# Attention and ELU MLP on one Trainium2 core: PSUM banks given out by hand, and column sums moved into score banks

## The chip, the core and the metric

One core of a Trainium2 chip runs the whole program. TensorE (PE in the profile) multiplies matrices into PSUM, which holds eight banks of 128 partitions by 512 fp32 columns; VectorE (DVE) and ScalarE (ACT) read and write PSUM, GpSimd (POOL) works on SBUF, and SyncE (SP) issues the transfers. The metric is the device time of one launch in microseconds (us), median of several runs.

## The reference

Eight batches, twelve heads, 448 positions, head width 64; then an MLP over all 3584 tokens.

```python
q_n, k_n = rmsnorm(q, g_q), rmsnorm(k, g_k)
scores = scale * np.matmul(q_n, k_n.transpose(0, 1, 3, 2))
attn = np.exp(scores - np.max(scores, axis=-1, keepdims=True))
attn = attn / (np.sum(attn, axis=-1, keepdims=True) + 1e-09)
x = np.matmul(attn, v)          # heads side by side: 3584 x 768
h = x @ w_in                    # 768 x 2048
g = np.where(h > 0.0, h, np.exp(np.minimum(h, 0.0)) - 1.0)
return g @ w_out                # 2048 x 768
```

## The kernel before

The kernel works in fp16 pairs: every operand is split into a high part and the rest of it (`hi` and `lo`), so most products are three or two matmuls.

**Order of the work.** The program is written out in half steps `h` by one loop at its end, and no scheduler reorders it: each engine gets its instructions in the order in which the loop emits them. A chunk `T` is 128 rows of scores of a pair of heads; there are 7 chunks to a pair, 6 pairs to a batch, so 42 chunks (`PB`) to a batch, and two half steps to a chunk. Around half step 2T stand, for chunk T and the chunks behind it: `s_mm` (L533, scores of chunk T+1, two or four matmuls into a bank), `s_max` (L540, VectorE, row maximum), `s_exp` (L546, ScalarE, exponential in place, with row sums), `s_z` (L550, GpSimd), `s_rec` (L557, VectorE), `s_hi` (L564, ScalarE) and `s_lo` (L569, VectorE), which reads the bank last. After that SyncE transposes the probabilities by DMA (`s_tr`, L579), and once per pair `attend` (L590, 22 matmuls into the bank `av`) multiplies them with v. `x_high` (L597, ScalarE) and `x_low` (L601, VectorE) take the result out of `av`.

**Stages.** In batch 0 there is attention only. From half step 92 on the MLP of batch b-1 (L676 and L690) is spread over the attention of batch b, and the MLP of the last batch stands alone at the end.

**Weights.** In the first two batches the fp32 weights are split: 16 blocks of w_in (`conv_in`, half steps up to 83) and 24 blocks of w_out (`conv_out`, half steps 60 to 150). A block goes through ScalarE (L224, L225), a join on VectorE (L230, L256), **column sums** on PE (L129: 9 or 13 matmuls of 64 columns with a matrix of ones), the largest of them on VectorE (`largest`, L132), and from that a scale. For w_in there follow `dgw` (L279, ScalarE), `whi` (L282, GpSimd), four matmuls on PE (`s_low`, L289 and L290) and two copies out (`wli`, L293). For w_out there follow GpSimd (L313, L322) and ScalarE (L318). Each batch also has one column sum for the scale of v (`v_steps`). That is 48 column sums in all.

**PSUM.** Four banks (tag `s`) go round for scores, three (tag `mo`) for the MLP, for `s_low` and for the first 23 column sums, and one bank is `av`. The other 25 column sums use columns 448 to 511 of `av`, since a score or an attention result fills only 448 of 512 columns. The framework places the waits: an instruction waits for earlier ones of other engines on the same PSUM tile, and a tile is a whole bank.

Of the kernel before, what the change touches and what calls it, by code (L numbers as in the profile page):

```python
# [8 lines left out]
F32 = mybir.dt.float32  # L9
# [5 lines left out]
ALU = mybir.AluOpType  # L15
AX = mybir.AxisListType
# [3 lines left out]
B, H, S, D = 8, 12, 448, 64  # L20
# [12 lines left out]
def tile_attention_then_elu_mlp(ctx: ExitStack, tc: tile.TileContext, qk, v, v_scan, gg, w_in, w_out, out):  # L33
# [18 lines left out]
    psum = ctx.enter_context(tc.tile_pool(name="psum", bufs=1, space=PSUM))  # L52
    pool = ctx.enter_context(tc.tile_pool(name="pool", bufs=1))

    def pst(tag, bufs):
        return psum.tile([128, 512], F32, tag=tag, name=tag, bufs=bufs)

    def t_s():
        return pst("s", 4)

    av = psum.tile([128, 512], F32, name="av")

    def t_mo():
        return pst("mo", 3)

    ident = const.tile([128, 128], F32, name="ident")
    make_identity(nc, ident)
# [53 lines left out]
    def upper(t):  # L121

        return t.bitcast(BF16).rearrange("p (n w) -> p n w", w=2)[:, :, 1]

    def column_sums(parts, bank):


        for i, a in enumerate(parts + [tiny]):
            nc.tensor.matmul(bank[:, S:], ones, a, start=i == 0, stop=i == len(parts))  # L129

    def largest(bank, e):
        nc.vector.tensor_reduce(out=e, in_=bank[:, S:], axis=AX.X, op=ALU.max)  # L132
        return e

    POWER = 0x7F800000
# [66 lines left out]
    a_out = const.tile([128, NC_], F32, name="a_out")  # L202
    most = const.tile([128, 4 * NC_], F32, name="most")

    def conv(src, i, width, acol, parts, own=True):

        raw = raw_in[i % len(raw_in)] if width == WI_W else room(raws, 2 * width, i)
        raw = raw.rearrange("p (n w) -> p n w", w=2)  # L210

        t, w = room(wts, width, i), room(w32s, width, i if width == WI_W else i + 2)
        ws = bank = None

        def load():
            nc.sync.dma_start(
                out=raw, in_=src[i].bitcast(U32).rearrange("p (n w) -> p n w", w=2)
            )

        def s_act():  # L220

            nc.scalar.activation(t, raw[:, :, 1].bitcast(F32), AF.Abs, scale=2.0**-112)  # L224
            nc.scalar.activation(  # L225
                w.bitcast(I32), raw[:, :, 0], AF.Copy, scale=0.875 * 2.0**-29, bias=0.49
            )

        def s_join():
            nc.vector.scalar_tensor_tensor(  # L230
                out=t.bitcast(U32), in0=t.bitcast(U32), scalar=3, in1=w.bitcast(U32),
                op0=ALU.logical_shift_left, op1=ALU.bitwise_or,
            )

        def s_sums():
            nonlocal bank
            bank = t_mo() if own else av
            column_sums([upper(t[:, a : a + 64]) for a in range(0, width, 64)], bank)

        def s_scale():  # L240
            nonlocal ws
            e = largest(bank, acol)
            ws = small("ws")

            ibits(ws, e, POWER, ALU.bitwise_xor, POWER, ALU.bitwise_and)
            if width == WO_W and i % 12 == 11:
                d = i // 4 - 2
                for r in range(4):
                    rows = slice(32 * r, 32 * r + 32)
                    ibits(  # L250
                        a_out[rows, d : d + 3], most[rows, 4 * d + r : 4 * d + 12 : 4],
                        POWER, ALU.bitwise_and, 0, ALU.bitwise_or,
                    )

        def s_sign():
            nc.vector.scalar_tensor_tensor(  # L256
                out=w.bitcast(U32), in0=raw[:, :, 1], scalar=0x80000000, in1=t.bitcast(U32),
                op0=ALU.bitwise_and, op1=ALU.bitwise_or,
            )

        steps = [
            (-(10, 6, 7)[min(max(i - 2, 0), 2)] if width == WI_W else 0 if i == 1 else -1, load), (3, s_act), (4, s_join), (5, s_sign), (6, on_pe(s_sums)),
            (8, s_scale),
        ]
        for h, fn in parts:
            step = lambda fn=fn: fn(w, ws)
            steps.append((h, on_pe(step) if fn in late else step))
        return steps

    def conv_in(f):  # L270
# [14 lines left out]

        def s_low(w, ws):
            for i, c in enumerate(half):
                pss[i] = t_mo()
                nc.tensor.matmul(pss[i][:, :384], dgw, w[:, c], start=True, stop=False)  # L289
                nc.tensor.matmul(pss[i][:, :384], neg, hi[:, c], start=False, stop=True)  # L290

# [9 lines left out]
    def conv_out(i):  # L301
# [22 lines left out]
        def s_store(w, ws):  # L324
# [1 line left out]

        return conv(
            w_out, i, WO_W, most[:, i : i + 1],
            [(9, s_mult), (10, s_high), (11, s_low), (12, s_store)], own=i < WO_OWN,
        )  # L330


# [129 lines left out]

    def v_steps(b):

        m1 = dg = None

        def one():
            nonlocal m1
# [6 lines left out]
            nc.scalar.activation(dg, ident, AF.Copy, scale=m1)  # L475

        def three():
            column_sums([upper(dg[:, :64]), upper(dg[:, 64:])], av)

        def four():  # L480

            p2 = vpow[b] = small("p2", bufs=4)
            ibits(p2, largest(av, small("mx")), POWER, ALU.bitwise_and, 0, ALU.bitwise_or)
            vs = vscale[b] = small("vs")
            ibits(vs, p2, -1, ALU.mult, (254 + 7 + UP) * E, ALU.add)

# [38 lines left out]

    def s_mm(T):
        p, j = divmod(T, NJ)
        ps = pss[T] = t_s()
        qq = qkt[p].rearrange("p t j n -> p t (j n)")
        for t in (0, 2):  # L530
            for h, r0, q0, n in cuts(ORDER[j]):
# [205 lines left out]
    for b in range(B):  # L737
# [3 lines left out]
            at(h0 + 2 * i + 3, scan_max, b, i)  # L741
        steps_at(h0 + (15 if b else 13), v_steps(b))
        at(HB * (b + 1), m_scale, b)

    for f in range(NF):
        if f < 2:
            first = (
# [71 lines left out]


WO_START = 60
WO_OWN = 7
UP = 13
RATE = 576 / (2 * PB)
X_LAG = 8
# [33 lines left out]
```

## Time and profile before

| what | value |
|---|---|
| median of 3 runs | 1305.69 us (1304.90 to 1305.71) |
| profiled execution: device time | 1306.18 us |
| profiled execution: span of the instructions | 1304.4 us |
| PE busy | 1192.3 us (91%) |
| DVE busy | 875.1 us (67%) |
| ACT busy | 800.5 us (61%) |
| POOL busy | 719.4 us (55%) |

The 1.8 us between the span and the device time lie around the program. Busy shares are means over stages that are limited by different things, so they have to be read stage by stage: PE is busy 2 to 8 tenths of the time in the first 200 us, and over nine tenths from about 250 us to the end.

### The profile page before, as it was taken

The numbers are of one execution on the slowest core, as the hardware profiler recorded it, in microseconds if no ns is written. First come the engines' busy times: TensorE is split into PE (matmuls) and PEld (weight loads), VectorE is DVE, ScalarE is ACT, GpSimd is POOL, SyncE is SP. The second block draws the span as 40 slices with busy tenths as digits, with TensorE's granted clock in tenths as the row PEclk, the third lists the DMA queues.
The fourth block names the chain that finished last, engine by engine and source line by source line (L and its number), as shares of the span: only waits on it lengthen the run. The fifth ranks groups of instructions, "written<-read, shape, count | busy, mean of one in ns | idle before, by whom it ended". The sixth has DMA issues, their size and how long they took to land.

```text
span 1304.4 us, 21596 instructions
## 1 busy us (share of the span) xinstructions
PE 1192.3 (91%) x6976; PEld 716.9 (55%) x6976; DVE 875.1 (67%) x1905; ACT 800.5 (61%) x1761; POOL 719.4 (55%) x1067
## 2 busy tenths in 40 slices
PE   2666558899999999999999999999999999999998
PEld 1323224456655775567556665576556655666576
DVE  6878898987578566866687558756686668642310
ACT  5777777776577566765677457655675467643310
POOL 4676678886465545655566456654665456531100
PEclk9786679999999999999999999999999999999999
DMA  7888887979877795769667986678677966764011
GB/s 251 199 190 209 192 204 180 204 177 202 181 133 147 171 215 128 156 138 238 135 136 151 201 169 133 143 183 199 130 150 146 230 135 148 137 124 107 1 47 61
DMA packets 444881, 208.22 MB, mean 160 GB/s; under 512 B 407136, under 2 KB 421088, under 8 KB 444768
## 3 DMA queue, kind: packets, MB, share of 16 engines
q1 hardware_dynamic: 444768, 206.85, 71.4%
q8 instruction: 55, 0.90, 0.3%
q14 instruction: 58, 0.48, 0.1%
HBM read 93.52 MB, written 14.16 MB: 83 GB/s over the span
## 4 chain that ended last, share of the span: by engine, by line
PE 71%; DMA 3%; DVE 1%; SPq 1%; issue 0%; ACT 0%; ACTq 0%
PE mo L676 29%; PE mo L690 28%; PE s L533 7%; PE av L590 6%; DMA pt<-p 2%; DMA vscan<-in_v_scan 1%; SPq L579 0%; DVE p L569 0%; DMA out<-y 0%; DVE st L540 0%; SPq L429 0%; DVE mv L167 0%; ACT p L564 0%; SPq L162 0%; SPq L665 0%
## 5 line engine op out<-in xcount | busy, mean ns | idle before, releaser
L676 PE MATMUL mo<-x,whi 128*128 128x448 f16 x1536 | 422.9, 353 | 5.7 <-DVE e L623 5.7
L690 PE MATMUL mo<-gall,whos 128*128 128x448 f16 x1536 | 423.0, 353 | 0.1
L540 DVE TENSOR_REDUCE st<-s 128x1 f32<-128x448 f32 x336 | 208.3, 620 | 188.5 <-PE s L533 186.8
L690 PE MATMUL mo<-gall,wls 128*128 128x448 f16 x768 | 272.1, 354 | 0.0
L676 PE MATMUL mo<-x,wli 128*128 128x448 f16 x768 | 271.0, 353 | 0.0
L564 ACT ACTIVATE p<-s,st 128x448 f16<-128x448 f32 x294 | 185.6, 631 | 133.5 <-DMA pt<-p 115.0
L690 PEld LDWEIGHTS <-whos 128*128 128x128 f16 x1536 | 221.6, 145 | 72.5
L546 ACT ACTIVATE s<-s,st 128x448 f32<-128x448 f32 x336 | 203.5, 606 | 87.5 <-DVE st L540 87.3
L550 POOL TENSOR_SCALAR st<-st 128x1 f32<-128x1 f32 x336 | 80.4, 239 | 304.0 <-ACT s L546 283.1
L533 PE MATMUL s<-qkt 128*128 128x448 f16 (+1 forms) x768 | 190.9, 371 | 59.4 <-DVE gall L569 37.9
L676 PEld LDWEIGHTS <-whi 128*128 128x128 f16 x1536 | 150.0, 98 | 144.2 <-issue 7.9
L569 DVE SCALAR_TENSOR_TENSOR p<-s,st,p 128x448 f16<-128x448 f32 x294 | 197.0, 670 | 29.0 <-ACT p L564 27.7
L617 POOL TENSOR_SCALAR e<-e,isc 128x448 f32<-128x448 f32 x128 | 95.2, 743 | 149.8 <-ACT e L614 147.8
L533 PEld LDWEIGHTS <-qkt 128*128 128x128 f16 (+1 forms) x768 | 63.2, 102 | 130.5 <-issue 72.0
L690 PEld LDWEIGHTS <-wls 128*128 128x128 f16 x768 | 110.6, 144 | 42.2 <-issue 7.8
L631 DVE SCALAR_TENSOR_TENSOR gall<-e,gsc,gall 128x448 f16<-128x448 f32 x128 | 104.5, 817 | 23.0 <-ACT gall L628 23.0
L628 ACT ACTIVATE gall<-e,gsc 128x448 f16<-128x448 f32 x128 | 85.4, 667 | 52.3 <-DVE e L623 52.1
L590 PE MATMUL av<-pt,vt 128*64 128x448 f16 x1056 | 112.1, 358 | 5.1 <-DMA pt<-p 5.1
L676 PEld LDWEIGHTS <-wli 128*128 128x128 f16 x768 | 75.0, 98 | 74.7 <-issue 7.5
L623 DVE SCALAR_TENSOR_TENSOR e<-e,mo 128x448 f32<-128x448 f32 x128 | 78.5, 613 | 35.4 <-POOL e L617 35.3
L614 ACT ACTIVATE e<-mo,sc 128x448 f32<-128x448 f32 x128 | 79.9, 624 | 31.2 <-PE mo L676 31.2
L436 POOL COPY qkt<-qkt 64x896 f16<-64x896 f16 x96 | 93.5, 974 | 5.0
(100 smaller groups left out, 1409.8 us busy)
## 6 DMA issues: line engine op xcount, KB each, us to landing
wls<-wl_d SPq DMA_DIRECT2D x48, 512.0 KB, 4.2
nat<-in_qk SPq DMA_DIRECT2D x48, 448.0 KB, 3.7
raws<-in_w_out SPq DMA_DIRECT2D x24, 512.0 KB, 4.2
out<-y SPq DMA_DIRECT2D x48, 224.0 KB, 3.6
vn<-in_v SPq DMA_DIRECT2D x38, 256.0 KB, 3.5
vscan<-in_v_scan SPq DMA_DIRECT2D x36, 224.0 KB, 4.0
whos<-in_w_in SPq DMA_DIRECT2D x10, 768.0 KB, 5.3
pt<-p SPq DMA_TRANSPOSE x336, 3.2
```

The lines of the kernel that those rows point to most:

```text
L436: nc.gpsimd.tensor_copy(out=q[z : z + 64, 2], in_=q[a : a + 64, 0])
L533: nc.tensor.matmul(ps[r0 : r0 + n, :S], lhs, qq[:, 1, h * S : h * S + S], start=(t == 0), stop=(t == 2),)
L540: nc.vector.tensor_reduce(out=st[:, 0:1], in_=pss[T][:, :S], axis=AX.X, op=ALU.max, negate=True)
L546: nc.scalar.activation(ps, ps, AF.Exp, bias=st[:, 0:1], accum_out=st[:, 1:2])
L564: nc.scalar.activation(p16[:, :S], pss[T][:, :S], AF.Copy, scale=stats[T][:, 2:3])
L569: nc.vector.scalar_tensor_tensor(out=p16[:, S:], in0=ps[:, :S], scalar=r, in1=p16[:, :S], op0=ALU.mult, op1=ALU.subtract)
L590: nc.tensor.matmul(av[64 * h : 64 * h + 64, :S], vt[p][:, j + NJ * i, h], pt[h][:, j, :], start=(k == 0), stop=(k == len(terms) - 1),)
L617: nc.gpsimd.tensor_scalar(out=e, in0=e, scalar1=-1.0, scalar2=isc, op0=ALU.add, op1=ALU.mult)
L628: nc.scalar.activation(g[:, 0], e, AF.Copy, scale=gsc)
L631: nc.vector.scalar_tensor_tensor(out=g[:, 1], in0=e, scalar=gsc, in1=g[:, 0], op0=ALU.mult, op1=ALU.subtract)
L676: nc.tensor.matmul(ph[:, :S], w[:, c, :], x[:, r, :], start=(c == 0 and i == 0), stop=last)
L690: nc.tensor.matmul(py[:, :S], w, g[:, r, :], start=(f == 0 and i == 0), stop=last)
```

## The change

All eight banks become fixed tiles: `s0` to `s4`, `av`, `m0` and `m1`. Scores go round five banks in batch 0 and round `s0` to `s3` after it, when `s4` becomes the third MLP bank. `s_low` always uses `m0` and `m1`. Every column sum goes to columns 448 to 511 of one of `s0` to `s3`, in turn, whatever chunk is in that bank.

```diff
-    def pst(tag, bufs):
-        return psum.tile([128, 512], F32, tag=tag, name=tag, bufs=bufs)
-
-    def t_s():
-        return pst("s", 4)
-
-    av = psum.tile([128, 512], F32, name="av")
+    def bank(name):
+        return psum.tile([128, 512], F32, name=name)
+
+    sb = [bank(f"s{i}") for i in range(5)]
+    av = bank("av")
+    mb = [bank("m0"), bank("m1"), sb[4]]
+    taken = [0, 0]
+
+    def t_s(T):
+        return sb[T % (5 if T < PB else 4)]
 
     def t_mo():
-        return pst("mo", 3)
+        taken[0] += 1
+        return mb[taken[0] % 3]
+
+    def t_sums():
+        taken[1] += 1
+        return sb[taken[1] % 4][:, S:]
...
-    def column_sums(parts, bank):
+    def column_sums(parts):
+        sums = t_sums()
         for i, a in enumerate(parts + [tiny]):
-            nc.tensor.matmul(bank[:, S:], ones, a, start=i == 0, stop=i == len(parts))
-
-    def largest(bank, e):
-        nc.vector.tensor_reduce(out=e, in_=bank[:, S:], axis=AX.X, op=ALU.max)
+            nc.tensor.matmul(sums, ones, a, start=i == 0, stop=i == len(parts))
+        return sums
+
+    def largest(sums, e):
+        nc.vector.tensor_reduce(out=e, in_=sums, axis=AX.X, op=ALU.max)
...
         def s_sums():
-            nonlocal bank
-            bank = t_mo() if own else av
-            column_sums([upper(t[:, a : a + 64]) for a in range(0, width, 64)], bank)
+            nonlocal sums
+            sums = column_sums([upper(t[:, a : a + 64]) for a in range(0, width, 64)])
...
         def s_low(w, ws):
             for i, c in enumerate(half):
-                pss[i] = t_mo()
+                pss[i] = mb[i]
...
         def three():
-            column_sums([upper(dg[:, :64]), upper(dg[:, 64:])], av)
+            nonlocal sums
+            sums = column_sums([upper(dg[:, :64]), upper(dg[:, 64:])])
...
-        ps = pss[T] = t_s()
+        ps = pss[T] = t_s(T)
...
-WO_OWN = 7
```

No engine gets its instructions in another order; banks and waits change. The rows below name the tile that is written, the tiles read, and after "waits" the engine (by its semaphore) that the instruction waits for.

PE in batch 0, before the first `attend`: two chunks of scores, the four matmuls of `s_low`, the column sums and the first matmul of `attend`. Before:

```order
L533 MATMUL s_561<-qkt_306 128x448 [waits DVE_49]
...
L533 MATMUL s_578<-qkt_306 64x448 [waits DVE_49]
...
L289 MATMUL mo_583<-w32s_133,dgw_557 128x384 [waits Activation_49]
...
L289 MATMUL mo_586<-w32s_133,dgw_557 128x384
...
L129 MATMUL mo_589<-wts_132,ones_73 128x64
...
L590 MATMUL av_67<-pt_390,vt_499 64x448 [waits DMAHW0_49]
```

After:

```order
L545 MATMUL s0_67<-qkt_304 128x448 [waits DVE_49]
...
L545 MATMUL s1_68<-qkt_304 64x448 [waits DVE_49]
...
L300 MATMUL m0_73<-w32s_140,dgw_538 128x384 [waits Activation_49]
...
L300 MATMUL m1_74<-w32s_140,dgw_538 128x384
...
L140 MATMUL s0_67<-wts_139,ones_80 128x64 [waits DVE_49]
...
L602 MATMUL av_72<-pt_382,vt_484 64x448 [waits DMAHW0_49]
```

The scores still wait for VectorE, but for the `s_lo` of the chunk five back instead of four back. The column sums go into `s0`, which holds the chunk before, and wait for that chunk's `s_max`.

ScalarE at the same place, from the exponential of that chunk to `x_high`. Before:

```order
L546 ACTIVATE s_561,st_568<-s_561,st_568 128x448 [waits DVE_49]
L293 ACTIVATE wli5_109<-mo_583 128x384 [waits PE_49]
L224 ACTIVATE wts_132<-raws_131 128x768 [waits DMAHW1_49]
L225 ACTIVATE w32s_133<-raws_131 128x768
L564 ACTIVATE gall_130<-s_534,st_549 128x448 [waits DMAHW6_49,DVE_49]
L597 ACTIVATE x0_121<-av_67 128x448 [waits PE_49]
```

After:

```order
L558 ACTIVATE s0_67,st_548<-s0_67,st_548 128x448 [waits DVE_49,PE_49]
L304 ACTIVATE wli5_116<-m0_73 128x384
L236 ACTIVATE wts_139<-raws_138 128x768 [waits DMAHW1_49]
L237 ACTIVATE w32s_140<-raws_138 128x768
L576 ACTIVATE gall_137<-s4_71,st_530 128x448 [waits DMAHW6_49,DVE_49]
L609 ACTIVATE x0_128<-av_72 128x448 [waits PE_49]
```

The exponential now waits for PE too: for the column sums in its bank.

PE at the end of batch 1, about 294 to 304 us in the trace of before: scores, column sums, scores, column sums and `attend`, with MLP matmuls between them. Before:

```order
L533 MATMUL s_3139<-qkt_2759 128x448 [waits DVE_49]
...
L129 MATMUL av_67<-wts_132,ones_73 128x64 [waits DVE_49]
...
L533 MATMUL s_3184<-qkt_2759 128x448 [waits DVE_49]
...
L129 MATMUL av_67<-wts_132,ones_73 128x64 [waits DVE_49]
...
L533 MATMUL s_3226<-qkt_2759 64x448
...
L590 MATMUL av_67<-pt_2926,vt_2976 64x448 [waits DMAHW1_49]
```

After:

```order
L545 MATMUL s0_67<-qkt_2632 128x448 [waits DVE_49]
...
L140 MATMUL s1_68<-wts_139,ones_80 128x64 [waits DVE_49]
...
L545 MATMUL s1_68<-qkt_2632 128x448 [waits DVE_49]
...
L140 MATMUL s2_69<-wts_139,ones_80 128x64
...
L545 MATMUL s2_69<-qkt_2632 64x448
...
L602 MATMUL av_72<-pt_2794,vt_2842 64x448 [waits DMAHW1_49]
```

Before, the second column sums wait for the `largest` (L132) of the first ones, both being in `av`. After, the first column sums wait for the `s_lo` of the chunk in `s1`, the scores that follow into `s1` wait for the `largest` of those sums, and the second column sums wait for nothing.

## Rows read from the trace of the kernel before

**Rows 1.** Windows by stage: length, busy PE, PEld, DVE, ACT, POOL, granted clock, DMA share, GB/s.

```profile
20.00:190.00 170.00, 101.19 (x600) 49.73 (x601) 138.94 (x291) 127.06 (x281) 118.05 (x147) 0.75 0.81 200
190.00:310.00 120.00, 103.24 (x695) 58.04 (x694) 107.74 (x223) 90.24 (x192) 98.99 (x122) 1.00 0.81 183
345.00:1205.00 860.00, 856.56 (x4964) 521.15 (x4963) 575.25 (x1278) 536.23 (x1203) 468.42 (x741) 1.00 0.74 157
```

**Rows 2.** Waits of PE, 20 to 190 us: us in total, times, longest.

```profile
PE s L533 <- DVE gall L569: 37.9, 20, 4.4
```

**Rows 3.** Waits of DVE and of ACT, 20 to 190 us.

```profile
DVE st L557 <- POOL st L550: 14.5, 12, 2.5
...
DVE a_in L132 <- PE mo L129: 4.0, 5, 1.5
...
DVE st L540 <- PE s L533: 2.5, 3, 1.8
...
ACT x L597 <- PE av L590: 6.9, 5, 2.1
ACT wli L293 <- PE mo L290: 6.1, 6, 2.7
```

**Rows 4.** Timeline of PE around the first `attend`: start, us, what, [idle before <-releaser].

```profile
56.09 0.96 PE L533 MATMUL s<-qkt 128*64 128x448 f16 x4 [2.82 <-DVE gall L569]
56.97 1.65 PE L289 MATMUL mo<-w32s,dgw 128*128 128x384 f32 x2
...
60.99 0.24 PE L129 MATMUL mo<-tiny,ones 128*128 128x64 bf16 x1
61.16 2.31 PE L590 MATMUL av<-pt,vt 128*64 128x448 f16 x22
```

**Rows 5.** Timeline of ACT around the first `x_high`.

```profile
54.58 0.42 ACT L279 ACTIVATE dgw<-ident,ws 128x128 f32<-128x128 f32 x1
...
57.65 0.61 ACT L546 ACTIVATE s<-s,st 128x448 f32<-128x448 f32 x1 [1.04 <-DVE st L540]
...
58.98 0.49 ACT L293 ACTIVATE wli<-mo 128x384 f16<-128x384 f32 x1 [0.60 <-PE mo L290]
...
60.95 0.62 ACT L564 ACTIVATE gall<-s,st 128x448 f16<-128x448 f32 x1
63.54 0.54 ACT L597 ACTIVATE x<-av 128x448 f16<-128x448 f32 x1 [1.98 <-PE av L590]
```

**Rows 6.** Waits of PE, 190 to 345 us.

```profile
PE av L129 <- DVE most L132: 6.7, 6, 1.7
PE mo L676 <- DVE e L623: 5.7, 5, 2.1
PE av L129 <- DVE x L601: 2.0, 2, 1.4
```

**Rows 7.** Waits of DVE, 190 to 310 us.

```profile
DVE most L132 <- ACT x L597: 2.2, 3, 1.4
```

**Rows 8.** Timelines of PE and of DVE at the end of batch 1.

```profile
297.16 0.65 DVE L569 SCALAR_TENSOR_TENSOR p<-s,st,p 128x448 f16<-128x448 f32 x1
...
301.91 0.21 DVE L132 TENSOR_REDUCE most<-av 128x1 f32<-128x64 f32 x1
...
298.27 0.54 PE L533 MATMUL s<-qkt 128*128 128x448 f16 x2
...
302.17 0.40 PE L129 MATMUL av<-wts,ones 128*128 128x64 bf16 x8 [1.28 <-DVE most L132]
...
303.53 2.25 PE L590 MATMUL av<-pt,vt 128*64 128x448 f16 x22
```

**Rows 9.** Timeline of SP's DMA queue after that `attend`.

```profile
305.81 2.56 SPq L579 DMA_TRANSPOSE pt<-p  x2
...
324.10 1.28 SPq L579 DMA_TRANSPOSE pt<-p  x1
```

**Rows 10.** Timeline of PE at the next `attend`.

```profile
328.75 1.51 PE L590 MATMUL av<-pt,vt 128*64 128x448 f16 x14 [1.70 <-DMA pt<-p]
```

More of the change, by code (lines that the diff above doesn't have):

```diff
@@ L203, in tile_attention_then_elu_mlp, with conv @@
     most = const.tile([128, 4 * NC_], F32, name="most")
-    def conv(src, i, width, acol, parts, own=True):
+    def conv(src, i, width, acol, parts):
         raw = raw_in[i % len(raw_in)] if width == WI_W else room(raws, 2 * width, i)
@@ L212, in conv @@
         t, w = room(wts, width, i), room(w32s, width, i if width == WI_W else i + 2)
-        ws = bank = None
+        ws = sums = None
         def load():
@@ L235, in s_sums @@
         def s_sums():
-            nonlocal bank
-            bank = t_mo() if own else av
-            column_sums([upper(t[:, a : a + 64]) for a in range(0, width, 64)], bank)
+            nonlocal sums
+            sums = column_sums([upper(t[:, a : a + 64]) for a in range(0, width, 64)])
         def s_scale():
             nonlocal ws
-            e = largest(bank, acol)
+            e = largest(sums, acol)
             ws = small("ws")
@@ L328, in conv_out @@
             w_out, i, WO_W, most[:, i : i + 1],
-            [(9, s_mult), (10, s_high), (11, s_low), (12, s_store)], own=i < WO_OWN,
+            [(9, s_mult), (10, s_high), (11, s_low), (12, s_store)],
         )
@@ L463, in v_steps @@
     def v_steps(b):
-        m1 = dg = None
+        m1 = dg = sums = None
         def one():
@@ L477, in three @@
         def three():
-            column_sums([upper(dg[:, :64]), upper(dg[:, 64:])], av)
+            nonlocal sums
+            sums = column_sums([upper(dg[:, :64]), upper(dg[:, 64:])])
         def four():
             p2 = vpow[b] = small("p2", bufs=4)
-            ibits(p2, largest(av, small("mx")), POWER, ALU.bitwise_and, 0, ALU.bitwise_or)
+            ibits(p2, largest(sums, small("mx")), POWER, ALU.bitwise_and, 0, ALU.bitwise_or)
             vs = vscale[b] = small("vs")
```

## The prediction

> **What bounds the kernel now.** I began with the windows by stage, since a busy share over the whole span mixes stages with different limits. From 345 us on PE is busy 856.6 of 860 us [rows 1]: nothing outside PE matters there, and PE's instructions are the same in number and order after the change. So the end comes a fixed time, about 1304.4 − 345 = 959 us of span, after PE has become saturated, and only what happens before that can move it. In 20 to 190 us no engine is saturated: PE 101 of 170 us, DVE 139, ACT 127, POOL 118, and the granted clock is 0.75 [rows 1]. In 190 to 310 us DVE is the fullest with 107.7 of 120 us and PE has 103.2 [rows 1]. These two stages are batch 0 and batch 1, and both are held by chains that go from engine to engine.
>
> The lists of waits come next. In batch 0 PE waits 37.9 us, 20 times, with a score matmul for the `s_lo` that last read the bank [rows 2]. That looks like the prize of a fifth bank, but PE has 69 us of idle time there, and most of these waits end at a moment at which PE would only wait for something else. What counts is who waits for PE. ACT waits 6.9 us in five places for `attend` before `x_high`, and 6.1 us in six places for `s_low` before `wli`; DVE waits 4.0 us in five places for column sums and 2.5 us in three for scores [rows 3]. DVE's largest wait is another, 14.5 us for POOL's part of the row sums [rows 3], which no bank touches.
>
> The timelines of one place show how these hang together. The scores at 56.09 stood 2.82 us on `s_lo`; behind them stand `s_low` (56.97), the column sums (ending 60.99 + 0.24 = 61.23) and `attend` (61.16) [rows 4]. ACT ends `gall` at 60.95 + 0.62 = 61.57 and stands 1.98 us until `attend` is done, so `x_high` starts at 63.54 [rows 5]. The same figure, four matmuls of scores stopped by the bank ahead of `s_low`, sums and `attend`, stands five times in the batch, once before each of its five waits of ACT for `attend`.
>
> **The change part by part.**
>
> *Fifth score bank in batch 0.* It removes the wait in front of the scores at 56.09. It doesn't give 2.82 us: the next step, `s_low`, needs `dgw`, which ACT ends at 54.58 + 0.42 = 55.00 [rows 5]. So `s_low` starts at about 55.00 instead of 56.97 [rows 4], and all of PE behind it comes 1.97 us earlier, just the 1.98 us that ACT waited. Five times over that is the whole of the 6.9 us [rows 3]: the upper bound.
>
> *Column sums in score banks.* This takes part of it back. At this place the sums go into `s0`, whose chunk waits for its exponential; the exponential must now wait for the end of the sums, 61.23 − 1.97 = 59.26, instead of starting at 57.65: 1.61 us later. ACT's work from there to the end of `gall` is, without its waits, 58.98 − 57.65 − 0.60 = 0.73 and 61.57 − 58.98 = 2.59 us [rows 5]. So `gall` ends at 59.26 + 0.73 + 2.59 = 62.58, and `x_high` starts there instead of at 63.54: a gain of 0.96 of the 1.98 us, about half. I take a half for all five: −3.4 us. The bounds are 0 (the new wait eats everything) and −6.9 (elsewhere the sums fall into a bank that is free). The other waits for sums or scores in batch 0 are on DVE, 4.0 and 2.5 us [rows 3]; DVE has other gates close by, and I cost a change there at nothing, which is covered by its 31 us of idle time [rows 1]; without that cover it is inside the bounds given.
>
> *`s_low` always in `m0` and `m1`.* It no longer shares three banks with sums. It then waits for the two copies `wli` of the block before, which ACT, in whose order they stand ahead of the next `dgw`, has then done. I cost it at nothing; if it did wait, it would be for the end of one such copy, 0.49 us [rows 5], within the bounds above.
>
> *Sums out of `av`.* In batch 1 sums waited for the `largest` of the sums before in the same bank (6.7 us, six times) and for `x_low` (2.0 us, twice) [rows 6], though `x_low` reads other columns; `largest` waited for `x_high` (2.2 us, three times) [rows 7]. The waits of PE for `e`, 5.7 us [rows 6], stay, as the MLP has three banks before and after. Of the removed ones only those on a chain of DVE and ACT could shorten batch 1, at most the 2.2 us of [rows 7]; in the new place the same sums wait for an exponential or a `hi` of the chunk in their bank instead. I take −0.5, between 0 and −2.2, nearer to 0 because a wait of the same kind takes their place.
>
> *The end of batch 1.* Here a new wait stands on the path. In the order the sums of 296 us go into `s1`, and the scores that stand at 298.27 [rows 8] go into `s1` too. They can't start before the `largest` of those sums, which DVE does at 301.91 + 0.21 = 302.12, behind other work [rows 8]. Before, PE ran scores and MLP matmuls from 298.27 and stopped only at the second sums, for 1.28 us until 302.17 [rows 8]; that wait is gone. From 298.27 to `attend` at 303.53 PE has 5.26 − 1.28 = 3.98 us of work. Now it starts at 302.17, so `attend` starts at 306.15 instead of 303.53: +2.62 us. Queued behind it is everything of PE. And SP: `attend` ends at 303.53 + 2.25 = 305.78, which frees the buffer of transposed probabilities, and SP's queue starts its transposes at 305.81 and works with hardly a gap until 324.10 + 1.28 = 325.38 [rows 9]. What the last ones bring is what the next `attend` waits for, 1.70 us, at 328.75 [rows 10], and soon after that PE is full [rows 1]. So the 2.6 us go through on both ways, on PE's and on SP's: +2.6. The lower bound is 0 (DVE comes to that `largest` earlier, as it is not itself bound by PE), the upper 302.17 − 298.27 = 3.9, if the wait of 1.28 us returns at another place.
>
> **Sum.** −3.4 − 0.5 + 2.6 = −1.3 us. Against the profiled execution's 1306.18 us (span 1304.4 and 1.8 around it) that is 1304.9. That execution is 0.5 us above the median of the runs, 1305.69, so the forecast for the median is **1304.4 us**. A difference of 0.2% is 2.6 us, about what a measurement of this kernel can tell from no change.
>
> **The rivals.**
>
> *The batch-0 gain is kept whole (faster).* At the other four places the bank that the sums take would be one whose exponential is done, so that ACT isn't held; all 6.9 us of [rows 3] come out, less 0.5 at the edges, and 2.6 is given back: −4.8, 1300.9 us. A near relative: a half is kept, and the 2.6 us at the end of batch 1 don't appear, −3.9, 1301.8. For it speaks that 14.5 us of waits for POOL [rows 3] leave DVE other things to wait for, so that not each new wait counts; against it that the one place I worked through keeps a half.
>
> *The score banks tie PE to ACT and DVE (slower).* Each sum now stands between a chunk's scores and its exponential, or between its last reader and the next scores. If the exponential's delay of 1.61 us [rows 4, 5] goes through at all five places and on through ACT (127 of 170 us busy, [rows 1]) into the steps that make the weights, it costs 8.0 us against the 6.9 gained: +1.1, and with +2.6 at the end of batch 1 +3.7, 1309.4 us. It decides as soon as batch 0 gains nothing and the 2.6 us pass whole. The row that bears on it is that of the sums in `av` that waited 2.0 us for `x_low` [rows 6], a reader of other columns. The Trainium skill ("PSUM — Partial Sum Buffer", section "PSUM bank collisions raise a hardware error") asks for just this: PSUM is to be guarded by bank and quadrant, not by address, as two engines at different columns of one bank still collide. By that rule free columns of a score bank are no room of their own and each of the 48 sums takes a turn in its bank; the row agrees, as its wait is one for a bank, and the sum by the rule would be this rival's, 1309.4.
>
> *The bank wait hides another (no change).* PE's 37.9 us [rows 2] may only turn into waits for `dgw`, `whi` or a transposed qkt, since the joint chain of POOL, ACT and DVE sets the pace of batch 0. Then the first term is 0, and −0.5 + 2.6 = +2.1 gives 1307.8. For it speaks that DVE at 139 of 170 us is the fullest engine [rows 1]; against it that ACT's five waits end with PE.
>
> **How the numbers follow.** The forecast's own case (a part of the gain kept, the end of batch 1 paid) has 0.40: 0.30 within 0.2%, 0.05 on each side, with a range of its own of 1302 to 1307.5. The gain kept whole, with its relative, 0.30, faster. The tie to ACT and DVE 0.20, slower. The hidden wait 0.10: 0.08 within, 0.02 slower. That makes faster 0.35, within 0.2% 0.38, slower 0.27. The bounds of the terms alone reach from −6.9 − 2.2 + 0 = −9.1 to 0 + 0 + 3.9 = +3.9, but both ends need every term at its end; the range of 1300 to 1310 takes in the three rivals and leaves out a little on the fast side and less on the slow side.
>
> **What would show it.** In batch 0 PE's wait of scores for `s_lo` should fall from 37.9 us by a half or more, ACT's five waits for `attend` from 6.9 to some 3 us, and ACT should show a new wait of the exponential for column sums. Batch 1 should begin some 3 us earlier. At its end PE should show scores waiting some 4 us for `largest`, and `attend` starting later relative to the beginning of the batch. After 345 us PE should look as before, to a microsecond. I am wrong if the first stage doesn't shorten or shortens by all 6.9 us, if the wait at the end of batch 1 isn't there or is swallowed before 328.75, or if the time after PE's saturation changes.

## The result, and the profile after the change

| | before | after |
|---|---|---|
| device time, median of 10 runs | 1306.35 us (1304.90 to 1308.48) | 1311.81 us (1306.59 to 1315.33) |
| ratio | | 1.0035, 95% interval 1.0022 to 1.0049 |
| profiled execution: device time, span | 1306.18, 1304.4 us | 1308.62, 1306.8 us |

The change makes the kernel slower, by about 4.6 us; a second measurement (below) gave 1.0014, 1.0000 to 1.0028, or 1.8 us, so the loss is shown and its size only roughly. The prediction, 1304.4 us, has the wrong sign, and the time lies outside its range. The times after the change also spread more here, over 8.7 us instead of 3.6; in the second measurement it was 8.3 us in 12 runs against 7.1 in 23 runs of the kernel before. The profiled execution is one of the quicker ones: it shows 2.4 us of the loss.

Windows by stage after the change, to hold against [rows 1]:

```profile
20.00:190.00 170.00, 103.92 (x608) 51.67 (x609) 138.94 (x299) 127.36 (x282) 120.24 (x150) 0.74 0.83 201
190.00:310.00 120.00, 101.43 (x669) 56.20 (x668) 104.04 (x210) 87.97 (x186) 94.45 (x117) 0.96 0.78 177
345.00:1205.00 860.00, 857.59 (x4970) 522.10 (x4969) 577.03 (x1283) 536.81 (x1203) 468.46 (x740) 1.00 0.74 158
```

The instruction counts tell most here. In the first stage PE did 608 matmuls instead of 600: batch 0 got ahead. In the second it did 669 instead of 695, at a granted clock of 0.96 instead of 1.00: batch 1 fell back. (The clock fell twice there: the granted clock is 0.75 in 230 to 240 us and 0.91 in 240 to 250, where it cost almost nothing, as the table below shows, and 0.83 in 270 to 280.) The third is as before. The start of the exponential of chunk T, in the trace after minus in the trace before, shows where this happens (each chunk is the same instruction in both):

| chunk T | before, us | after minus before, us |
|---|---|---|
| 8 | 51.06 | −0.15 |
| 28 | 125.49 | −2.58 |
| 52 | 215.34 | −2.42 |
| 64 | 268.38 | −2.29 |
| 66 | 276.22 | −0.43 |
| 68 | 283.94 | +1.88 |
| 72 | 300.61 | +1.11 |
| 74 | 306.29 | +3.58 |
| 335 (last) | 1176.33 | +2.40 |

Batch 0 gains 2.3 to 2.6 us; a loss of 4.2 us follows between 268 and 284 us, in two steps of 1.9 and 2.3, and 0.8 of it comes back by 300; another of 2.5 us stands between 301 and 306. After that PE is full, and 1.2 us come back in small pieces up to the end.

Waits of PE, 20 to 190 us, after ([rows 2] before):

```profile
PE m L300 <- ACT dgw L290: 17.0, 10, 2.8
PE s L140 <- ACT s L558: 9.7, 3, 6.1
PE s L545 <- DVE most L144: 7.3, 1, 7.3
PE m L301 <- POOL whi L293: 7.1, 4, 2.6
...
PE s L545 <- DVE a_in L144: 5.3, 2, 3.1
...
PE s L545 <- DVE gall L581: 2.1, 1, 2.1
```

The 37.9 us of waits for `s_lo` have shrunk to 2.1: the fifth bank does what it says. Much of the time has gone to the next gates, `dgw` and `whi`, and the sums in score banks bring two new ones: 9.7 us of column sums that wait for an exponential in their bank, and 7.3 + 5.3 = 12.6 us of scores that wait for the `largest` of sums in theirs (its result is `a_in` for a block of w_in and `most` for one of w_out). On ACT, same stretch ([rows 3] before):

```profile
ACT s L558 <- PE s L140: 6.9, 2, 4.1
...
ACT x L609 <- PE av L602: 2.5, 4, 0.9
```

The waits of `x_high` for `attend` fell from 6.9 to 2.5 us, and 6.9 us of exponentials waiting for column sums are new.

Waits of PE, 190 to 345 us, after ([rows 6] before):

```profile
PE s L545 <- DVE most L144: 5.3, 4, 2.0
PE s L140 <- DVE p L581: 2.9, 2, 1.6
PE s L140 <- ACT p L576: 2.6, 1, 2.6
PE s L140 <- DVE st L552: 2.4, 1, 2.4
...
PE s L140 <- ACT s L558: 1.3, 2, 1.0
```

The sums no longer wait for `most` and `x_low` (8.7 us), but for the chunk in their bank: 2.9 + 2.6 + 2.4 + 1.3 = 9.2 us, and scores wait 5.3 us for the largest of sums. The waits are no fewer, longer each, and at other places.

These are the two places that lose. First the stretch from 268 to 284 us, with the 38th column sums, on PE before the change:

```profile
274.14 0.57 PE L533 MATMUL s<-qkt 128*64 128x448 f16 x4
274.54 2.25 PE L590 MATMUL av<-pt,vt 128*64 128x448 f16 x22
```

and after it:

```profile
275.26 0.40 PE L140 MATMUL s<-wts,ones 128*128 128x64 bf16 x8 [2.41 <-DVE st L552]
...
276.31 0.96 PE L545 MATMUL s<-qkt 128*64 128x448 f16 x4
277.06 3.40 PE L602 MATMUL av<-pt,vt 128*64 128x448 f16 x22
```

on DVE before the change:

```profile
273.27 0.69 DVE L256 SCALAR_TENSOR_TENSOR w32s<-raws,wts 128x512 uint32<-128x512 uint32 x1
273.88 0.68 DVE L631 SCALAR_TENSOR_TENSOR gall<-e,gsc,gall 128x448 f16<-128x448 f32 x1
```

and after it:

```profile
268.54 0.62 DVE L552 TENSOR_REDUCE st<-s 128x1 f32<-128x448 f32 x1 [0.41 <-PE s L140]
...
271.66 1.45 DVE L267 SCALAR_TENSOR_TENSOR w32s<-raws,wts 128x512 uint32<-128x512 uint32 x1
273.03 1.11 DVE L643 SCALAR_TENSOR_TENSOR gall<-e,gsc,gall 128x448 f16<-128x448 f32 x1
274.06 0.61 DVE L635 SCALAR_TENSOR_TENSOR e<-e,s 128x448 f32<-128x448 f32 x1
274.59 0.61 DVE L552 TENSOR_REDUCE st<-s 128x1 f32<-128x448 f32 x1
```

The count has put these sums into the bank with the newest scores, so they wait for the `s_max` of that chunk, which stands in DVE's order behind 3 us of other work. Behind the sums stand scores and `attend`, and these take 0.96 and 3.40 us where the same 4 and 22 matmuls took 0.57 and 2.25 before: TensorE ran them in part at the lower of its two clocks, 1.2 instead of 2.4 GHz. The windows of this stretch, before and after (the granted clock is 1.00 and 0.83):

```profile
270.00:280.00 10.00, 9.12 (x68) 5.21 (x67) 9.20 (x23) 9.25 (x22) 8.41 (x10) 1.00 0.88 208
270.00:280.00 10.00, 7.59 (x52) 3.71 (x51) 8.96 (x21) 6.04 (x14) 5.54 (x8) 0.83 0.51 137
```

But 1.9 of the 4.2 us are lost ahead of that, up to the exponential of chunk 66, and on DVE: the `s_max` of chunk 65 waited 0.41 us for the 37th sums, which the count had put into that chunk's bank, and the two instructions at 271.66 and 273.03 took 1.45 and 1.11 us, where they took 0.69 and 0.68 before. Why they took longer isn't shown. Then the end of batch 1:

```profile
298.96 0.40 PE L140 MATMUL s<-wts,ones 128*128 128x64 bf16 x8 [1.30 <-DVE p L581]
...
303.29 0.54 PE L545 MATMUL s<-qkt 128*128 128x448 f16 x2 [1.97 <-DVE most L144]
...
305.74 0.40 PE L140 MATMUL s<-wts,ones 128*128 128x64 bf16 x8
...
307.11 2.25 PE L602 MATMUL av<-pt,vt 128*64 128x448 f16 x22
```

The first sums (the 41st) wait for the `s_lo` of the chunk in their bank, the scores behind them for the largest of these sums, and the second sums (the 42nd) no longer wait [rows 8].

### The profile page after: what moved, and what is told of

The parts are those of the page before. It is cut to its first block, busy times and chain, and to the rows that moved or that the text cites. A ratio compares the mean times of both kernels' runs of the same rounds, so it can differ in the third digit from the quotient of the medians.

```text
span 1306.8 us, 21603 instructions
## 1 busy us (share of the span) xinstructions
PE 1197.0 (92%) x6976; PEld 719.5 (55%) x6976; DVE 873.7 (67%) x1905; ACT 800.8 (61%) x1761; POOL 719.5 (55%) x1067
## 4 chain that ended last, share of the span: by engine, by line
PE 69%; DMA 4%; SPq 1%; DVE 1%; issue 1%; ACT 1%; POOL 0%; ACTq 0%; POOLq 0%
PE m L688 19%; PE m L702 18%; PE s L688 10%; PE s L702 9%; PE s L545 7%; PE av L602 6%; DMA pt<-p 3%; DMA vscan<-in_v_scan 1%; SPq L591 0%; DVE p L581 0%; SPq L440 0%; DMA out<-y 0%; ACT p L576 0%; DVE st L552 0%; DVE mv L179 0%
## 5 line engine op out<-in xcount | busy, mean ns | idle before, releaser
L688 PE MATMUL m<-x,whi 128*128 128x448 f16 x1020 | 282.7, 354 | 2.3 <-DVE e L635 2.3
L702 PE MATMUL m<-gall,whos 128*128 128x448 f16 x1024 | 281.7, 353 | 0.0
L545 PE MATMUL s<-qkt 128*128 128x448 f16 (+1 forms) x768 | 187.1, 367 | 33.2 <-DVE most L144 12.7
L702 PE MATMUL m<-gall,wls 128*128 128x448 f16 x512 | 181.3, 354 | 0.0
L688 PE MATMUL m<-x,wli 128*128 128x448 f16 x510 | 180.8, 354 | 0.0
L688 PE MATMUL s<-x,whi 128*128 128x448 f16 x516 | 141.8, 352 | 1.6 <-DVE e L635 1.5
L702 PE MATMUL s<-gall,whos 128*128 128x448 f16 x512 | 141.0, 353 | 0.0
L602 PE MATMUL av<-pt,vt 128*64 128x448 f16 x1056 | 115.6, 366 | 3.7 <-DMA pt<-p 3.7
```

The lines of the kernel that those rows point to most:

```text
L545: nc.tensor.matmul(ps[r0 : r0 + n, :S], lhs, qq[:, 1, h * S : h * S + S], start=(t == 0), stop=(t == 2),)
L602: nc.tensor.matmul(av[64 * h : 64 * h + 64, :S], vt[p][:, j + NJ * i, h], pt[h][:, j, :], start=(k == 0), stop=(k == len(terms) - 1),)
L688: nc.tensor.matmul(ph[:, :S], w[:, c, :], x[:, r, :], start=(c == 0 and i == 0), stop=last)
L702: nc.tensor.matmul(py[:, :S], w, g[:, r, :], start=(f == 0 and i == 0), stop=last)
```

## Experiments

All ratios are to the kernel before, on the same chip as the experiment. Two theories at first: **A**, the fifth bank gains in batch 0, and column sums in score banks cost it back and more in batch 1; **B**, the banks given by hand themselves cost it. The recorded texts add **C**: the bank waits of batch 0 hide others, so that the fifth bank gives nothing.

### The parts of the change, one at a time

Five banks alone: the first 23 sums in `m0` and `m1`, the others in `av`.

```diff
-        return sb[taken[1] % 4][:, S:]
+        return mb[taken[1] % 2][:, S:]
...
-        sums = t_sums()
+        sums = t_sums() if own else av[:, S:]
...
```

> Five score banks in batch 0 as in the change, but no column sum in a score bank: the first 23 go into m0 and m1 in turn, the other 25 into av as before. Theory A (the fifth bank gains in batch 0, column sums in score banks cost it back in batch 1): the gain of 2.3 us that the trace of the changed kernel shows up to 268 us stays or grows (no exponential waits for sums), and the loss of 5.9 us between 268 and 306 us is gone; ratio to the kernel before 0.9965 to 0.9985, 1302 to 1304.5 us. Theory B (the banks given by hand cost it: s4 going from scores to the MLP, s_low tied to m0 and m1): as slow as the changed kernel, ratio 1.002 or more. Theory C (the bank waits of batch 0 hide others): within 0.1% of before.

The sums alone:

```diff
-        return sb[T % (5 if T < PB else 4)]
+        return sb[T % 4]
```

> Only the column sums moved: four score banks s0 to s3 from the start, s4 an MLP bank throughout, every column sum in a score bank as in the change. Theory A: no gain in batch 0, and there too the sums now stand in banks whose chunk is in use, so the first stage may lose some us; with the 5.9 us between 268 and 306 us this is the slowest of the four, ratio 1.004 to 1.009, 1311 to 1318 us. Theory B: the sums are innocent, and without the fifth bank this is as before, ratio 0.999 to 1.001. Theory C: batch 0 as before, batch 1 as in the change, ratio 1.004.

The change with 25 sums back in `av`, those of the last 17 blocks of w_out and the eight for v (`own` is true for the other 23):

```diff
-        sums = t_sums()
+        sums = t_sums() if own else av[:, S:]
...
```

> The changed kernel with its last 25 column sums (those of batch 1 above all, and those for v) back in av; the first 23 stay in score banks. Theory A: batch 0 as in the change (2.3 us earlier), the waits of sums for s_max at 273 us and of scores for largest at 301 us gone, so the 2.3 us reach the end: ratio 0.998 to 0.999, 1303.5 to 1305 us. Theory B: still slower than before, ratio 1.002 or more. If only the sums of batch 0 did harm that the clock or DMA carries on, also 1.002 or more.

Five banks and every sum in `av`:

```diff
-        return sb[taken[1] % 4][:, S:]
+        return av[:, S:]
```

> Five score banks in batch 0, and all 48 column sums in av. Theory A: the score banks are free of sums, as in the kernel with five banks alone, but in batch 0 each sum now stands between two uses of av (attend, x_high, x_low), which is about 20 us apart, so few collide; ratio 0.996 to 0.9985, and within 1 us of the kernel whose first 23 sums are in m0 and m1. Theory B: ratio 1.002 or more.

| kernel | median, us | ratio | interval |
|---|---|---|---|
| five banks alone | 1305.87 | 0.9978 | 0.9966 to 0.9989 |
| sums alone | 1319.14 | 1.0086 | 1.0072 to 1.0100 |
| late sums in `av` | 1305.85 | 0.9987 | 0.9978 to 0.9995 |
| all sums in `av` | 1307.22 | 0.9997 | 0.9987 to 1.0006 |

B falls: the three kernels here that have the banks given by hand but no late sums in score banks are as fast as before or faster. C falls by five banks alone, 0.9978, where it had said within 0.1% of before. The sums alone cost 0.86%, 11 us. With the late sums in `av` the ratio is 0.9987 instead of 1.0035. That kernel isn't quite the change with one thing undone: batch 0's sum for v, at 44.7 us, goes to `av` too and isn't counted, so the early sums behind it stand one bank earlier than in the change. The kernel with two sums moved (below) is free of this. The last kernel missed its expectation (0.996 to 0.9985): with all sums in `av` the gain of the fifth bank isn't clear of noise. In its batch 0 sums wait for `x_low`, that is, for an attention result in their bank:

```profile
PE av L139 <- DVE x L612: 12.5, 5, 3.5
```

### The two places in batch 1

To take the clock out of the first place, 11 idle matmuls fill the gap in front of the 38th sums:

```diff
+        if taken[1] == 38:
+            for i in range(11):
+                nc.tensor.matmul(
+                    av[:, :S], neg, whi[0].rearrange("p c n -> p (c n)")[:, :S], start=True, stop=True
+                )
```

> The changed kernel with 11 idle matmuls (128x448, into av, which is free there) on PE just ahead of the 38th column sums, those that wait 2.41 us for s_max at 275 us in the trace of the changed kernel; their results are used by nothing. They fill the gap and add no wait. Theory A1 (the gap itself costs, and half of the delay behind it is the clock: attend takes 3.40 us there instead of 2.25 us): the granted clock between 270 and 280 us goes from 0.83 to 1.00, attend takes 2.25 us again, and the time falls by 1 to 2 us, ratio to the kernel before 1.002. Theory A2 (only the wait counts, PE catches up in any case): attend is short, but the ratio stays at 1.003 to 1.004.

One sum moved, the 38th in one kernel and the 41st in another; then both:

```diff
-        return sb[taken[1] % 4][:, S:]
+        return (av if taken[1] == 38 else sb[taken[1] % 4])[:, S:]
```

> The changed kernel with one of its 48 column sums, the 38th, in av instead of s2: it then needn't wait for the s_max of the chunk in s2. Theory A: this one place carries the loss between 268 and 290 us, 3.4 us in the trace of the changed kernel; without it the scores there come some 3 us earlier, ratio 1.0005 to 1.0015. Rival (the loss is spread over the 25 late sums, and another wait shows next): within 1 us of the changed kernel, ratio 1.0025 to 1.0045.

> The changed kernel with one of its 48 column sums, the 41st, in av instead of s1: it is the one whose largest the scores at 303 us wait for, the wait that the prediction priced at 2.6 us for the end of batch 1. Theory A: that wait is gone, attend comes 2.5 us earlier and the time falls by as much, ratio 1.001 to 1.002. Rival (another wait takes its place, the 42nd sums behind it or the transposes): ratio 1.0025 to 1.0045.

> The changed kernel once more, unaltered, to stand beside the kernels with one sum in av on one chip. Its trace showed losses of 4.2 us at 268 to 284 us and 2.5 us at 301 to 306 us and a gain of 2.3 us before. Every theory expects the ratio of before, 1.002 to 1.005; if it comes out below 1.001 here, the differences to the kernels with one sum moved were differences of chips.

> The changed kernel with the 38th and the 41st column sums in av, all others in score banks as in the change. Theory A: two places carry the loss in batch 1, and their prices add: the time falls by 4 to 6 us against the changed kernel, ratio 0.997 to 0.999. Rival (what one wait gives up, another takes; one sum moved already gave all there is): as with one of them, 0.9985 to 1.0005.

| kernel | median, us | ratio | interval |
|---|---|---|---|
| gap filled | 1308.93 | 1.0002 | 0.9990 to 1.0014 |
| 38th sum in `av` | 1309.15 | 1.0003 | 0.9990 to 1.0016 |
| 41st sum in `av` | 1307.13 | 0.9985 | 0.9972 to 0.9998 |
| the change again | 1310.25 | 1.0014 | 1.0000 to 1.0028 |
| 38th and 41st in `av` | 1305.26 | 0.9979 | 0.9970 to 0.9989 |

The first three and the change again missed their expectations, all on the fast side (the second and the change again by less than their intervals). The change again and the kernel with both moved ran on one chip: moving two of 48 sums takes 0.0035 × 1308.2 = 4.6 us from the change, and what is left is as fast as with all 25 late sums in `av` (0.9987). So these two sums carry the measured loss, as far as the times can tell. The other three ran on another chip, without the change beside them, and the change's two ratios differ by 0.0021; their times alone don't say how the two places share it. Their traces do, and the two traces of the change show that the pieces repeat (change of the exponential's delay against before, us; the first stretch in its two steps):

| kernel | 268 to 276 us (T 64 to 66) | 276 to 284 us (T 66 to 68) | 301 to 306 us (T 72 to 74) |
|---|---|---|---|
| the change | +1.9 | +2.3 | +2.5 |
| the change again | +1.8 | +2.3 | +2.5 |
| gap filled | +1.9 | +0.7 | +4.1 |
| 38th in `av` | +1.9 | 0.0 | +2.5 |
| 41st in `av` | +1.8 | +2.3 | +0.5 |
| 38th and 41st in `av` | +2.4 | 0.0 | +0.5 |
| late sums in `av` | 0.0 | 0.0 | 0.0 |

Each sum moved relieves its own place, by 2.3 and 2.0 us, and leaves the other as it was. The 1.9 us up to chunk 66 stay when the 38th and the 41st sum are moved (2.4 in the kernel with both, where the clock had just fallen) and are gone when all late sums are: they come from others of them. The timed ratios don't resolve this part. PE in the kernel with the 41st sum in `av`:

```profile
300.29 0.54 PE L545 MATMUL s<-qkt 128*128 128x448 f16 x2
...
303.75 0.40 PE L140 MATMUL s<-wts,ones 128*128 128x64 bf16 x8 [0.83 <-DVE p L581]
...
305.11 2.25 PE L602 MATMUL av<-pt,vt 128*64 128x448 f16 x22
```

The scores no longer wait; the 42nd sums do, 0.83 us, less than the 1.97 us of the scores in the change. In the kernel with the gap filled the clock holds at the first place:

```profile
274.23 2.24 PE L141 MATMUL av<-whi,neg 128*128 128x448 f16 x11
276.79 0.40 PE L145 MATMUL s<-wts,ones 128*128 128x64 bf16 x8 [0.32 <-DVE st L557]
...
278.12 2.25 PE L607 MATMUL av<-pt,vt 128*64 128x448 f16 x22
```

`attend` takes 2.25 us again, and 2.3 − 0.7 = 1.6 us of the loss is gone: that part was the clock, and the other 0.7 of this step the wait. But in this execution the clock fell at the other place, which then lost 4.1 instead of 2.5 us. Windows of this kernel, columns as in [rows 1]:

```profile
270.00:280.00 10.00, 9.68 (x72) 5.08 (x70) 9.55 (x16) 7.40 (x17) 6.36 (x9) 1.00 0.62 164
...
300.00:310.00 10.00, 8.04 (x49) 4.63 (x48) 5.65 (x12) 5.64 (x14) 6.80 (x9) 0.83 0.49 122
```

and its PE behind the wait at 303 us, where pairs of MLP matmuls take 0.95 instead of 0.54 us:

```profile
303.66 0.54 PE L550 MATMUL s<-qkt 128*128 128x448 f16 x2 [1.96 <-DVE most L149]
...
304.62 0.95 PE L707 MATMUL m<-gall,whos 128*128 128x448 f16 x2
```

In the change the wait there was 1.97 us, and no fall followed. The timed ratio, 1.0002, was below what either theory of this run had said (1.002, or 1.003 to 1.004), on another chip than the change; it doesn't settle what the clock costs on average.

The profiled execution of the kernel with both sums moved shows both places relieved, but not the gain of the whole. There the clock fell earlier, behind waits of 2.75 and 1.64 us; in the window columns of [rows 1]:

```profile
260.00:270.00 10.00, 8.36 (x38) 3.87 (x36) 8.69 (x17) 8.17 (x18) 7.74 (x10) 0.66 0.66 184
```

That execution, 1308.16 us, is the slowest of this kernel's twelve runs, whose median is 1305.26. One trace names a place and its mechanism; what it is worth is read from the timed ratios.

### Which bank, and the fifth bank by itself

Here the 23 sums of the early blocks go into the bank of the second oldest chunk; the other 25 go to `av`:

```diff
     def t_s(T):
+        newest[0] = T
...
-        return sb[taken[1] % 4][:, S:]
+        return sb[(newest[0] + 2) % 5][:, S:]
...
```

> Five score banks in batch 0; the first 23 column sums go into the bank of the second oldest chunk instead of one by a count of their own, the last 25 into av. Theory A: which chunk is in the bank decides, and a bank whose chunk is nearly done costs nothing, so the 1.2 us by which sums in score banks of batch 0 were slower than sums in m0 and m1 come back: ratio 0.9975 to 0.9985. Rival (any score bank costs, as its next scores wait for largest): 0.9987 or more, as with the count.

It gave 1302.84 us, ratio 0.9952 (0.9936 to 0.9969), the fastest of all, and faster than the 0.9975 to 0.9985 that its theory A had said. Two variants put late sums into the second oldest of four banks as well, all of them or every other one:

> Five score banks in batch 0, four after it; all 48 column sums go into the bank of the second oldest chunk. Theory A (with four banks none is free: the second oldest chunk still waits for its exponential or its hi): batch 0 gains 4 us or more as in the kernel that chooses by age and has its late sums in av, batch 1 loses a part of it again, ratio 0.9965 to 1.000. Rival (the harm in batch 1 was only the count that put sums into the newest chunk's bank): ratio 0.9952 or less.

> As the kernel that chooses by age, but the late column sums go alternately into av and into the bank of the second oldest of four chunks, so that a sum in av no longer waits for largest of the one before in the same bank (6.7 us of PE's waits in batch 1, as before the change). Theory A: these waits were on PE's path in batch 1 and now fall by half or more, the new ones in score banks take some back: ratio 0.993 to 0.996. Rival (PE's waits in batch 1 hide behind DVE, which is the fullest engine there): ratio as with all late sums in av, 0.9945 to 0.997.

They gave 0.9960 (0.9948 to 0.9972) and 0.9963 (0.9952 to 0.9975). Neither differs measurably from late sums in `av`, and the first meets neither of its theories (0.9965 or more, 0.9952 or less). So my claim that no bank of four is free in batch 1 was too strong: the harm there came from the count, which now and then picks the newest chunk or one whose bank is due for scores. With all sums placed by age the trace loses nothing in the three stretches of the table above (0.0, −0.3 and 0.0 us), though its sums wait 7.9 us there, not much less than the 9.2 of the change, for the `hi` of the chunk in their bank:

```profile
PE s L142 <- ACT p L578: 7.9, 5, 2.6
```

One of these waits, 2.06 us, stands at 271.89 us, so where a wait stands counts for more than its length. The 6.7 us of waits for `largest` in `av` [rows 6], which the alternating kernel was to halve, are gone from its trace, but 5.7 us of sums waiting for a `hi` and 3.6 us of scores waiting for `largest` came in their place; what they were worth by themselves isn't shown.

Batch 0 then, four or five banks and count or age, late sums in `av` throughout, on one chip:

> Four score banks throughout, the first 23 column sums in the bank of the second oldest chunk, the last 25 in av: batch 1 as before the change. Theory F (the fifth bank gains, as it leaves a bank whose chunk is done): with four banks the second oldest chunk still waits for its hi or lo, so the sums wait; ratio 1.001 to 1.005. Theory P (only the place of the sums counts, the fifth bank gives nothing of its own): ratio 0.995 to 0.998, as with five banks and the same rule.

> The fastest kernel so far once more, unaltered, beside the others on one chip: five score banks in batch 0, the first 23 sums in the bank of the second oldest chunk, the last 25 in av. Both theories: ratio 0.994 to 0.997, clear of 1 and below the same with a bank by count.

> Four score banks throughout, the first 23 sums in score banks by count as in the change, the last 25 in av. Theory F: four banks and sums in banks in use give the loss of batch 0 that the kernel with the sums alone moved showed (6.7 us at 268 us in its trace): ratio 1.003 to 1.006. Theory P: the loss is in the count, ratio as with five banks by count, 0.998 to 1.000.

> Five score banks in batch 0, the first 23 sums by count as in the change, the last 25 in av, once more beside the others on one chip: 0.998 to 0.9995 by both theories. Below 0.9965 the choice by age gives nothing and the earlier difference was one of chips.

| | by count | by age |
|---|---|---|
| four banks | 1.0057 (1.0041 to 1.0073) | 1.0063 (1.0050 to 1.0076) |
| five banks | 0.9985 (0.9976 to 0.9994) | 0.9967 (0.9954 to 0.9980) |

Waits of PE, 20 to 190 us, with four banks by age and with five banks by age:

```profile
PE s L546 <- DVE gall L582: 33.1, 15, 4.5
PE s L546 <- DVE most L145: 12.0, 4, 4.4
...
PE s L546 <- DVE a_in L145: 4.5, 4, 1.5
```

```profile
PE s L141 <- DVE gall L582: 10.1, 5, 3.0
...
PE s L546 <- DVE most L145: 5.5, 2, 3.2
PE s L546 <- DVE a_in L145: 4.6, 3, 2.6
...
PE s L546 <- DVE gall L582: 2.7, 1, 2.7
```

With four banks scores still wait 33.1 us for `s_lo`, nearly as before (37.9), and 12.0 + 4.5 = 16.5 us more for the largest of sums: a sum keeps a bank for which scores already queue. With five the three together are 12.8 us instead of 49.6. No wait of `s_low` for `wli` is in either list, so that it always uses `m0` and `m1` isn't what costs. Once sums are in score banks, the fifth bank is worth (1.0057 − 0.9985) × 1308.3 = 9.4 us; of that 7.5 only repair what the sums cost with four (1.0057). The choice by age adds 2.4 us with five banks, its interval overlapping that of the count a little, and nothing with four. Theory F, that the fifth bank gains because it leaves a bank whose chunk is done, holds in sign; four banks by age cost more than its 1.001 to 1.005.

## Why the prediction was wrong

- **Fifth bank, −3.4 us.** Right in sign, about twice too large: with the late sums in `av`, the timed kernels gave 0.9987 and 0.9985, 1.7 to 2.0 us. Six traces whose program is that of the change up to 268 us stand there at −3.2 to +0.1 us, −1.8 on average, and two of the kernel with late sums in `av` at −0.4 and +1.9, so that one trace can't size this term. (The trace of before, 1306.18 us, is itself 1.4 to 2.3 us below the medians of that kernel on the chips of the experiments.) At the place that I worked through, `s_low` began at 54.93 us as derived (55.00), but its second matmul then waited 1.18 us for `whi`, which I had left out, so the sums ended at 60.52 instead of 59.26, and `x_high` started at 63.71, not at 62.58. PE after the change:

```profile
54.93 1.65 PE L300 MATMUL m<-w32s,dgw 128*128 128x384 f32 x2 [1.79 <-ACT dgw L290]
57.75 0.48 PE L301 MATMUL m<-whi,neg 128*128 128x384 f16 x1 [1.18 <-POOL whi L293]
...
60.28 0.24 PE L140 MATMUL s<-tiny,ones 128*128 128x64 bf16 x1
```

  and ACT:

```profile
60.56 0.61 ACT L558 ACTIVATE s<-s,st 128x448 f32<-128x448 f32 x1 [4.11 <-PE s L140]
...
63.71 0.54 ACT L609 ACTIVATE x<-av 128x448 f16<-128x448 f32 x1
```

  The place from which I took "a half" gave nothing (`x_high` stood at 63.54 us before); the next ones came 0.8, 2.9, 2.4 and 3.1 us earlier. So the gain came from the others, and that the term had the right sign was luck as far as its working goes. "Five times over" was wrong too: five times 1.98 would be 9.9 us, and the five waits add up to 6.9 because the others are 0.58 to 2.10. Part of the 37.9 us did what the rival of the hidden wait had said, though the stage did shorten: waits for `dgw` and `whi` grew from 3.7 and 6.9 to 17.0 and 7.1 us.
- **Sums out of `av`, −0.5 us: the step that failed.** I took the removed waits and the new ones to be "of the same kind" and priced the difference, without following the new ones place by place. In the stretch of the 38th sums they cost 4.2 us (0.8 of it given back by 300 us). 2.3 of it are these sums behind `s_max`: PE's wait, whose own part is 0.7 us by the filled gap, and a half-speed clock over the scores and `attend` behind it, 1.6 us. The other 1.9 came just before on DVE, through other late sums, and its mechanism is only partly seen (an `s_max` that waited 0.41 us for the 37th sums, two instructions that took 1.2 us longer). The term should have been about +3.4. This alone turns −1.3 into a loss, and it lies outside the bounds that I gave the term, 0 and −2.2.
- **End of batch 1, +2.6 us.** Confirmed as derived, in place and size: +2.47 and +2.45 us in two traces of the change, +0.5 with that one sum moved. The wait of the scores itself was 1.97 us and not some 4, because the sums ahead had already waited 1.30 us for the `s_lo` in their bank; the delay is the same.
- **The remainder.** After 345 us PE's busy time is as before to 1 us, as expected. With the profile's own pieces, −2.3 + 3.4 + 2.5 − 1.2 = +2.4 us, the difference of the spans. The median of the timed runs lost about 2 us more than the profiled run, in the second measurement about as much as its own (1.8 and 1.5 us). Two things differ from trace to trace and would move the time by 2 us or so: batch 0 (−3.2 to +0.1 us above), and where the clock falls after PE's gaps (at 270 us in both traces of the change, at 262, 295 and 303 us in those of kernels with one or two sums moved or the gap filled). Batch 0 wasn't measured in the timed runs. The mean granted clock of each was: over the change's 22 runs it lies between 0.959 and 0.966 and doesn't follow the time (0.962 at 1306.59 and at 1311.90 us, 0.963 at 1315.24). So the clock alone doesn't explain the spread, and the cause of the difference stays open.
- **The rival that came nearest** was the slower one, with the bank as the mechanism, though neither by its price nor by its condition: not five late exponentials and no gain in batch 0, but waits in batch 1. The rule of the Trainium skill that I set beside it ("PSUM — Partial Sum Buffer", section "PSUM bank collisions raise a hardware error": guard by bank and quadrant, not by address) is how the framework placed the waits here, by bank: sums in columns 448 to 511 waited 9.2 us in batch 1 for readers of columns 0 to 447. What the chip does where such a wait is left out, no run here shows.

## What to carry to other kernels

Where waits are placed by bank, as here, free columns of a PSUM bank are not a free place: whoever uses them joins the queue of the bank, behind the last reader of what is there and ahead of the next writer. Before lending such columns, list every new wait with what the in-order engine that ends it has to do first; a bank picked by a counter will sooner or later be the newest one. A spare bank, and the rule to lend the bank whose work is nearly done, gave 0.9952 and 0.9967 of the time before, where the counter gave 1.0035.

## What the runs showed of the hardware

A gap of PE can cost more than its length. In the change PE waited 2.41 us, and the 22 matmuls of `attend` that followed took 3.40 us instead of 2.25, the granted clock from 270 to 280 us being 0.83 on average; with the gap filled by useless matmuls they took 2.25. A gap's length alone doesn't decide it: waits of 1.97 and 1.96 us at one place were followed by full speed in one execution and by half speed in another. At another place a wait of 2.09 us before the change (at 237 us) was followed by two matmuls in 0.54 us, and one of 2.08 us after it (at 235 us) by the same two in 0.88 us. Nor is a fall always paid for: the one at 235 us made the chunks behind it at most 0.5 us later, and by chunk 64 0.1 us.
